# Retention followed by an MLP mixer on one core: the wide product of batches 2 and 3 by seven block products, and the narrow product's seven with fewer sums outside PSUM

## The chip, the core and the metric

The kernel runs on one core of a Trainium2 chip. The core has a matrix engine (TensorE, PE in the profile), VectorE (DVE), ScalarE (ACT), GpSimd (POOL) and SyncE (SP), which run their own instruction streams and wait for each other through semaphores. Matmul results land in PSUM, which has eight banks of 128 x 512 float32; everything else lies in SBUF. The metric is device time in microseconds (us).

## What is computed

Four batches, eight heads, 768 steps, head width 64. First a recurrent retention, then an MLP mixer over tokens (768 to 256 to 768) and over channels (512 to 1536 to 512):

```python
for t in range(S):
    state = gamma[None, :, None, None] * state + np.einsum('bhd,bhe->bhde', k[:, :, t], v[:, :, t])
    y[:, :, t] = scale * np.einsum('bhd,bhde->bhe', q[:, :, t], state)
...
xt = x.transpose(0, 2, 1)                     # x: y with its heads side by side
h = np.maximum(xt @ w_tok1, 0.0) @ w_tok2
u = x + h.transpose(0, 2, 1)
h2 = np.maximum(u @ w_ch1, 0.0) @ w_ch2
return (u + h2).astype(np.float32)
```

`u @ w_ch1` is called the wide product here (512 to 1536 channels), `relu(...) @ w_ch2` the narrow one.

## The kernel before, in words

**Fronts.** For each batch b and pair of heads p (four pairs), `front` (L470) does the retention in six chunks of 128 steps and the token mixer: it scales k and q by their decay (L498, L500), turns k and q (L522, L524 on PE, or a DMA transpose on SP, L512), sums the states between chunks (L553 on PE, L563 and L565 on DVE, L573 and L575 for the cast r), multiplies q by k under a mask (L589; the masked copy `am`, L615 on DVE, or L602 on ACT with L607 on POOL), adds up y (L626, L634), and mixes tokens (L657, L677). It leaves u in float32 in X and in float16 in u16 (L644, L701), and u16 is turned into uT, [128 channels, 4, 768 tokens], by a DMA transpose (L715) or by PE.

**Backs.** For each batch, `back` (L739) has these steps. `widen(sh)` (L750), for each half of the tokens: for each of 12 tiles of 128 wide channels, four matmuls of 384 columns into one bank (L760), emitted two by two, then a relu into h by ACT (L776). h is one buffer of [128, 12, 384] for each half, and there are two such buffers. `narrow7(i0, i1)` (L816) takes two blocks of 128 tokens and multiplies [2 token blocks x 1536] by [1536 x 512] as 2 x 2 blocks with seven products instead of eight: sums of h blocks (`hs`, L835, DVE), sums of w_ch2 blocks (`wsum`, L944, once), seven products of six matmuls of 256 columns (L850) into halves of three banks, and the recombination by DVE sums (L867): partial sums kept in SBUF in `us`, and sums into X. After that ACT issues the output's DMA (L904). All four batches take seven products in the narrow step, except that the last two token blocks of batch 3 use the plain `narrow` (L783, matmuls at L797, sums at L806).

**What sets the order.** Each piece of work is an `Op` with the engines that may do it, planned costs, dependencies, and the buffers it takes and uses. `arrange` (L94) plans all of it as a list schedule: each engine takes the first ready op in the order of a written-out rank (PRECEDENCE, L251), with rooms of each buffer kind (BUFS, L311) and PSUM banks (BANKS, L313: fronts take banks 0 to 5, backs 4 to 7, those of batch 0 banks 3 to 7). Where an op may go to one of several engines, the plan takes the one that it expects to end first, with 800 ns added to DVE after 30 us. The program is emitted in the planned order, so at run time each engine's order is fixed. Loads are issued by POOL in the order of the list ORDER (L918), except the first k by SP; until 21 us, idle PE time is filled with matmuls on zeros (L967).

Buffers before, one line of the code (name = number of rooms):

```python
BUFS = dict(kf=1, k=4, q=4, v=4, k16=3, q16=2, kT=4, qT=4, U=2, r16=3, am=8, X=3, x16=4, h1=5, u16=3,
            uT=2, h2=2, hs=2, us=2)
```

Of the kernel before, what the change touches and what calls it, by code (L numbers as in the profile page):

```python
# [9 lines left out]
FP = mybir.dt.float32  # L10
# [12 lines left out]
class Op:  # L23
# [3 lines left out]
    def __init__(self, ops, prio, ways, deps=(), takes=(), uses=(), dma=None, after=(), behind=None, guard=0):  # L27
        self.prio, self.ways, self.dma, self.guard = prio, ways, dma, guard
        self.deps = [d for d in deps if d is not None]
        self.after = [d for d in after if d is not None]  # L30
        self.behind = behind
        self.takes = list(takes)
        for s in list(takes) + list(uses):
            s.users.append(self)
        self.n = len(ops)
        ops.append(self)
# [51 lines left out]
ENGINES = ("PE", "ACT", "DVE", "POOL", "SP")  # L88
FREE = dict(PE=300, ACT=2500, DVE=900, POOL=900, SP=750)


def arrange(ops, BUFS, BANKS, rank):
# [18 lines left out]
    landed = []  # L111
    t = 0.0
# [61 lines left out]
    while left:  # L174
        moved = False
        wake = INF
        for e in ENGINES:
# [4 lines left out]
            for o in w_:  # L182
# [20 lines left out]
                start[o.n], eng[o.n], begun[o.n], way_of[o.n], bank_of[o.n] = t, e, True, way, banks  # L203
                free[e] = t + way[1]
                if o.dma:
                    rings.add(e, o, t)
                    if e == "SP":
                        free[e] = max(t + way[1], rings.made["SP"][-3])
                else:
                    end[o.n] = t + way[2]  # L210
# [41 lines left out]
    "a7sobxu4amg9691jmwlfv8dy40jegv0id1brctk2abu22jwa1o7wcwi9h93p4srd0d3w8z9rvbq63zkynbegkm53vwm682qhecai0qwnjiny"  # L252
    "6nprc04c3ucqralmiummeyb9an4n58b6fsmlu929r9r74bbudiadx1m2skajdlbaujjjnpww4m8bki9ebfapry52pfu0ugt0jsvc6g17dwb3"
    "7kgwngc1pca2kpg5l7bwr6nlagfg7ti81022rpax5gwvubvokoayl9itr57lt4n3lglkm5sl1efl0htbr15w6qwh3ghrpn9uale6789q5hqy"
    "e4mnn1iefv9bk5cv328p3s5zaa0cv3ke38usjwbh2eiqw39kuyrbnaato05e0mf1p6s0irwzavh7iceoqw6fp07ol0tpp185wc25uxl49w97"
    "au1fligypb8xobtl8ludnw6ygon5a53ysy9gfd5tssq1lqa9w47js25o8tc6ci98t7lwhs6ikvq2dccbtm943obk6dqj6cuz5mv7bn1dfola"
    "rfc7r3lh30t2pkx50xncuiekcr0red64gb6o6sndfkoobg79lrqdixdh5kpxqk8oquj3rmt58d9hpuju939677hdbmph0n2u0odtjpjgj7ot"
    "63mbe76xohq5txtj3akx0j7v68wsd3gqhfjco9bs7a5dulv075fy1arqa1vfdgqfgjijwfmcrlp4af7y91ut5ve5gpjy74vyd9oxkw609s1p"
    "k8ha152q8krrpt1h494t6hnf3qg4encadz4uvh2lk1lywoddj2f7lj12ro72x4ur3e3r6l904z99h22ow7th5a86ckc3rk0t0zgla65i1ncz"
    "dbqcrj84upl5w248bv9yak4e9x953c1q76wt8emzszuf3np73d1r5yhjouowbjrzgr6rm1sq36s58v11rcjkm8ktuh8solco5cjb20nih8q8"  # L260
    "815ss97urhejg1ewv9wisd7m2zf6v26z1m4qdodj3jhpezfmumlolegas4chg888hmft9o8r6teuojpwee9ikn189jcjc53bx0p82sw9i3r0"
    "ah0e4jku4xds07emp5klvvfinkwduqhk2ttomawj2dq431cmb8e270s6plri37o762lvnq1c19vjd6k7fnfz3l6upy1vru8ivkial38moksr"
    "p9j8b2lxhgkb4yev0uhipgu5vu0kmq1i9dq98ghosnpq009mmu16t1lzq35bnsmd7b1zpmb0vr7ch0bisw4lqsguwmhvwxg69tbqdu5p9ft9"
    "03l1lsbl9cqi8f8afu5jdfpogfnecyopuvsa0bm46joy576k2foztdmvkhlt6b4gd0vlaspafeexi12acfmhe3gnaz0a0p7ig2drffae41o6"
    "mt14qn1xva02ggmsfqvprv7e73lddaip2nt6seqm5fh5u1w69l4io3iwuor43vpp0gtsvxsu0l4pucet243fp2r8nm8qilhuhte0jx7qw5si"
    "ikqpqa6vdnc98uifi0kr2vv11gi780tn51fj71o2hbsv7gcglnllel1sf5vdqqcd47nvini4javzwqtcqx65cearisksaclcl2hhqrfxa3q7"
    "kqtzj41um9613mwywlqo33rx27jneasmmed4wuefjldpk04osgs3aq44imawwk892hg3bt9po8l8f4uan8orbejf7smrpvtwfcbo3higvmk3"
    "4250x35r044h21qgti8cfrk63iwb0yioj5vibd2wvnc8dqhqttccj6h1dk2p46mje8s8ihc2gxdeaopjtrd74asbgcvgge4vhxoeno6wmxiy"
    "cpjdii7ftunzg7kzo1f8b1lpjmoad566fwj909gt4des8nf31bdv23a8n7ps13st2ch3jh0wmkgdd2058wnhtvi2mgk99vwpsfi6h4n0lunu"
    "83ql2kdxuw45kg3kqe87m71tp3qbfbkjhnt3e1r2o41yeqocbpw8bb7xpiuet8tqtgdme9miwecsgzpdf2jzrn92scovcl6au8oq7dmpw0n2"  # L270
    "qz7zbya0b5hy1k7n5qtkizmykcukcnrtibka6708cu56fhhc9n54ebj0tfm3idiv2rgin9pzpeod01gmj1vqh69znxuub7un8h0ffp35spn4"
    "w1jovsmont8jmfl67p06qv555xn6ehwgjrei28jv6mheepnrkdrg1lte2b2mcx5ulbon593tfave7hofkk6p4w393xta4fersjf0njogb4rw"
    "u6gh9ahzf9g0d87rjqkfreq00s0vv5nnhw8y2yc44ko5vtv4qt43jtosbcwrsxa46e4rv6bzs12x5lrshl26i5342ioiomtyk4x2shs75nu7"
    "m0gk1wgsu32g"
# [4 lines left out]
def kernel(  # L279
# [31 lines left out]
    BUFS = dict(kf=1, k=4, q=4, v=4, k16=3, q16=2, kT=4, qT=4, U=2, r16=3, am=8, X=3, x16=4, h1=5, u16=3,  # L311
                uT=2, h2=2, hs=2, us=2)
    BANKS = dict(first=range(0, 8), front=range(0, 6), back=range(4, 8), back0=range(3, 8))  # L313
    SEVEN = (0, 1, 2, 3)
    CLIP = (2, 3)
# [46 lines left out]
    gq = const_p.tile([P, NP, S // 2], FP, name="gq")  # L362
    since = const_p.tile([P, HC, P], FP, name="since")
# [3 lines left out]
    zero = const_p.tile([P, 384], F16, name="zero")  # L367
    g128 = [(1.0 - 2.0 ** (-5.0 - h)) ** P for h in range(H)]

    def prep(eng, cost, emit, deps=(), prio=(-20, 0, -1)):  # L370
        return Op(ops, prio, [(eng, cost, cost + 40, emit)], deps)
# [12 lines left out]
    lgs_op = prep("DVE", 900, emit, [away_op])  # L384
# [9 lines left out]
    def emit():  # L394
        nc.gpsimd.iota(since, pattern=[[0, HC], [1, P]], base=-MID, channel_multiplier=0,
                       allow_small_or_imprecise_dtypes=True)
    since_op = prep("POOL", 500, emit)
# [5 lines left out]
    lnh_op = prep("DVE", 600, emit)  # L403

    def emit():
        for p in range(NP):
            nc.scalar.activation(gq[:, p], since.rearrange("p i t -> p (i t)"), AF.Exp, bias=lnsc, scale=lnh[:, p:p + 1])
    gq_op = prep("ACT", 1900, emit, [since_op, lnh_op, lgs_op], (-20, 0, -1, 1))
# [5 lines left out]
    gp_op = prep("DVE", 600, emit, prio=(-20, 0, -1, 2))  # L414
# [9 lines left out]
    wc1 = [const_p.tile([P, NP, FW * P], F16, name=f"wc1_{i}") for i in range(3)]  # L424
    wc2 = const_p.tile([P, NF, C], F16, name="wc2")
    N2, K2 = C // 2, NF // 2
    wsum = const_p.tile([P, 4, K2, N2], F16, name="wsum")
    wops = {}
# [20 lines left out]
    def load(b, p, what):  # L449
# [3 lines left out]
        s = Slot("kf" if hard else what)  # L453
# [16 lines left out]
    def front(b, p):  # L470
# [4 lines left out]
        def op(ways, deps=(), takes=(), uses=(), late=0, behind=None):  # L475
# [3 lines left out]
            return Op(ops, pr, ways, deps, takes, uses, guard=200 if pe and not first else 0, behind=behind)  # L479
# [28 lines left out]
        def turn(src, dst, dep, mode):  # L508
# [17 lines left out]
            t = op(one("PE", (340, 500), emit), dep + [ident_op], [T], [src])  # L526
            if mode == "w":
                def emit():
                    d = tile_of(dst, [P, S], F16).rearrange("d (f p c) -> d f p c", f=2, c=NC)
                    o = T.tile[:, :S].rearrange("d (c f p) -> d f p c", f=2, c=NC)  # L530
                    w = gq[:, p:p + 1].rearrange("d o (p c) -> d o p c", c=NC).to_broadcast([P, 2, SH // NC, NC])
                    nc.vector.tensor_tensor(d, o, w, ALU.mult)
                return op(one("DVE", (870, 950), emit), [t, gq_op], [dst], [T])
# [21 lines left out]
        pp = op(one("PE", (290, 450), emit), kl + [vl, two_before], [ST], [K, V])  # L555
# [20 lines left out]
        rs = op(either(emit, ACT=(455, 555), POOL=(450, 510), DVE=(235, 320)), [prev], [RS], [US])  # L576
# [14 lines left out]
        if first:  # L591
            a2 = [op(one("PE", (200, 350), lambda f=emit, h=hf: f([h])), [kt, qt, two_before],
                     A4[2 * hf:2 * hf + 2], [KT, QT]) for hf in range(2)]
        else:
            a2 = 2 * [op(one("PE", (360, 480), lambda f=emit: f([0, 1])), [kt, qt, two_before], A4, [KT, QT])]
# [40 lines left out]
        y2 = op(one("PE", (200, 360), emit), [rs, kt, qt, y0], [], [QT, RS] + Y)  # L636
# [102 lines left out]
    def back(b):  # L739
# [10 lines left out]
        def widen(sh):  # L750
            H2 = H2s[sh]
            rel = []
            for ft in range(NF):
                A = Slot(BA)

                def emit(cts, sh=sh, ft=ft, A=A):
                    acc = tile_of(A, [P, 512], FP) if cts[0] == 0 else A.tile
                    w = wc1[ft // FW]
                    for ct in cts:
                        nc.tensor.matmul(acc[:, :SH], w[:, ct, (ft % FW) * P:(ft % FW + 1) * P],  # L760
# [20 lines left out]
            rels.append(rel)  # L781

# [33 lines left out]
        def narrow7(i0, i1):  # L816
# [23 lines left out]
            opened = set()  # L840

            def product(g, half, left, right, deps):
                opens = g not in opened
                opened.add(g)

                def emit():
                    acc = tile_of(banks[g], [P, 512], FP) if opens else banks[g].tile
                    l, r = left(), right()
                    for j in range(K2):
                        nc.tensor.matmul(acc[:, half], l[:, j], r[:, j], start=(j == 0),  # L850
                                         stop=(j == K2 - 1))
                return op(one("PE", (650, 810), emit), deps, [banks[g]] if opens else [],
                          [ha, hb, HS] if opens else [ha, hb, HS, banks[g]])

# [7 lines left out]

            def add(dst, a_, b_, deps, uses, takes=()):
                def emit(e):
                    if US.tile is None:
                        tile_of(US, [P, 3, N2], FP)
# [80 lines left out]
    for b in range(B):  # L947
        for p in range(NP):
            front(b, p)
# [50 lines left out]
```

## Time and profile before

| | |
|---|---|
| time, median of 3 runs | 197.39 us (196.89 to 197.91) |
| the profiled execution | 197.98 us, of it span 196.0 us |
| instructions | 5761 |
| busy: PE, PEld (weight loads), DVE, ACT, POOL | 185.5, 137.9, 130.6, 119.8, 86.5 us |
| wide matmuls L760 / narrow matmuls L850 | 384 / 462 |
| granted TensorE clock | 1.00 throughout |

The page splits the span into 40 slices of 4.9 us; a digit is an engine's busy share of a slice in tenths. A row of a group gives line, engine, operation, tile written and tiles read, shape, count, then busy time, mean ns of one, and the idle time before them with what ended it. A matmul's ns is its duration from start to modelled end; in a stream matmuls overlap, so the spacing of starts is shorter. The chain of waits is the path followed back from the last instruction; its pieces are start, duration, engine, tile, line. The view of busy time by stages gives, for each stretch, its length, busy time of PE, PEld, DVE, ACT and POOL with instruction counts, the granted clock, and DMA.

### The profile page before, as it was taken

The numbers are of one execution on the slowest core, as the hardware profiler recorded it, in microseconds if no ns is written. First come the engines' busy times: TensorE is split into PE (matmuls) and PEld (weight loads), VectorE is DVE, ScalarE is ACT, GpSimd is POOL, SyncE is SP. The second block draws the span as 40 slices with busy tenths as digits, with TensorE's granted clock in tenths as the row PEclk, the third lists the DMA queues.
The fourth block names the chain that finished last, engine by engine and source line by source line (L and its number), as shares of the span: only waits on it lengthen the run. The fifth ranks groups of instructions, "written<-read, shape, count | busy, mean of one in ns | idle before, by whom it ended". The sixth has DMA issues, their size and how long they took to land.

```text
span 196.0 us, 5761 instructions
## 1 busy us (share of the span) xinstructions
PE 185.5 (95%) x2374; PEld 137.9 (70%) x2374; DVE 130.6 (67%) x356; ACT 119.8 (61%) x266; POOL 86.5 (44%) x112
## 2 busy tenths in 40 slices
PE   7879689999999999899999999999999999999993
PEld 3447578666678898667569888865579976667772
DVE  6799785465999999830379999704239993006981
ACT  3852569987798456399789454788774404674000
POOL 8993679624677527672454883134302100000000
PEclk9999999999999999999999999999999999999999
DMA  6999999999999999999978799992200443000124
GB/s 107 155 184 187 177 203 173 185 193 189 137 156 133 139 168 186 164 215 185 142 76 82 138 169 164 258 125 40 43 0 3 147 113 146 0 0 3 54 107 161
DMA packets 94233, 25.53 MB, mean 130 GB/s; under 512 B 84352, under 2 KB 91264, under 8 KB 94208
## 3 DMA queue, kind: packets, MB, share of 16 engines
q0 software_dynamic: 67456, 13.18, 83.2%
q1 hardware_dynamic: 23152, 5.71, 20.9%
q10 hardware_dynamic: 3600, 6.29, 10.5%
q8 instruction: 18, 0.29, 0.6%
q14 instruction: 7, 0.06, 0.1%
HBM read 26.74 MB, written 6.29 MB: 169 GB/s over the span
## 4 chain that ended last, share of the span: by engine, by line
PE 73%; DVE 9%; DMA 5%; issue 4%; POOL 3%; ACT 3%; POOLq 0%; DVEq 0%
PE bank L760 31%; PE bank L850 20%; PE bank L677 4%; PE bank L657 4%; DMA k<-in_k_dram 3%; PE bank L589 3%; PE bank L797 2%; PE bank L626 2%; DMA uT<-u 2%; DVE U L565 2%; DVE hs L835 2%; PE bank L634 2%; PE bank L553 2%; DVE am L615 1%; POOL r L575 1%
## 5 line engine op out<-in xcount | busy, mean ns | idle before, releaser
L760 PE MATMUL bank<-uT,wc 128*128 128x384 f16 x384 | 69.7, 326 | 0.5 <-DMA uT<-u 0.5
L776 ACT ACTIVATE h<-bank 128x384 f16<-128x384 f32 x96 | 45.2, 494 | 20.5 <-PE bank L760 13.5
L760 PEld LDWEIGHTS <-wc 128*128 128x128 f16 x384 | 34.9, 98 | 20.7
L615 DVE TENSOR_TENSOR am<-bank,mask 128x384 f16<-128x384 f32 x48 | 24.6, 551 | 10.2 <-PE bank L589 10.1
L850 PEld LDWEIGHTS <-hs 128*128 128x128 f16 x264 | 25.0, 98 | 3.8 <-DVE hs L835 0.2
L701 POOL CAST u<-X 128x384 f16<-128x384 f32 x23 | 12.4, 561 | 34.3 <-issue 17.8
L850 PE MATMUL bank<-wsum,hs 128*128 128x256 f16 x198 | 26.2, 273 | 0.0
L867 DVE TENSOR_TENSOR X<-X,bank 128x256 f32<-128x256 f32 x55 | 21.6, 417 | 1.9 <-PE bank L850 1.3
L835 DVE TENSOR_TENSOR hs<-h 128x768 f16<-128x768 f16 x18 | 10.1, 568 | 18.7 <-ACT h L776 18.7
L850 PEld LDWEIGHTS <-h 128*128 128x128 f16 x198 | 18.8, 98 | 3.7 <-issue 0.7
L460 POOL DMA_DIRECT2D v<-in_v_dram x16 | 16.6, 1037 | 8.5 <-PE bank L626 5.1
L575 POOL TENSOR_SCALAR r<-U,gp 128x320 f16<-128x320 f32 x11 | 13.0, 1179 | 14.7 <-DVE U L565 13.5
L565 DVE SCALAR_TENSOR_TENSOR U<-U,gp,bank 128x64 f32<-128x64 f32 x64 | 17.8, 278 | 1.6
L867 DVE TENSOR_TENSOR X<-X,us 128x256 f32<-128x256 f32 x44 | 18.4, 441 | 0.2
L850 PE MATMUL bank<-wc,h 128*128 128x256 f16 x132 | 17.7, 273 | 0.0
L563 DVE COPY U<-bank 128x64 f32<-128x64 f32 x16 | 3.5, 221 | 20.9 <-PE bank L553 20.7
L644 ACT COPY X<-bank 128x384 f32<-128x384 f32 x31 | 14.2, 485 | 5.4 <-PE bank L677 5.3
L644 ACT CAST x<-bank 128x384 f16<-128x384 f32 x32 | 14.4, 481 | 4.9 <-PE bank L634 2.5
L460 POOL DMA_DIRECT2D k<-in_k_dram x15 | 15.7, 1048 | 0.8 <-ACT h L776 0.7
L677 PE MATMUL bank<-h,wt 128*128 128x64 f16 x384 | 15.2, 193 | 0.7 <-ACT h L666 0.7
L677 PEld LDWEIGHTS <-wt 128*128 128x128 f16 x384 | 13.9, 98 | 2.4 <-issue 0.9
L498 ACT ACTIVATE k<-k,gk 128x384 f16<-128x384 f16 x22 | 12.8, 612 | 0.9 <-DMA k<-in_k_dram 0.8
(71 smaller groups left out, 257.6 us busy)
## 6 DMA issues: line engine op xcount, KB each, us to landing
out_dram<-X ACTq DMA_DIRECT2D x23, 256.0 KB, 2.9
q<-in_q_dram POOLq DMA_DIRECT2D x16, 192.0 KB, 8.4
v<-in_v_dram POOLq DMA_DIRECT2D x16, 192.0 KB, 8.2
k<-in_k_dram POOLq DMA_DIRECT2D x15, 192.0 KB, 7.6
wc<-in_moe_w_ch_dram POOLq DMA_DIRECT2D x5, 512.0 KB, 11.8
wt<-in_moe_w_tok_dram POOLq DMA_DIRECT2D x2, 384.0 KB, 8.8
wc<-in_moe_w_ch_dram POOLq DMA_DIRECT2D x2, 256.0 KB, 10.3
kf<-in_k_dram SPq DMA_DIRECT2D x1, 384.0 KB, 3.6
```

The source lines that it names most:

```text
L460: (nc.sync if hard else nc.gpsimd).dma_start(out=tile_of(s, [P, 2, NC, D], FP if hard else F16), in_=src.rearrange("h (c p) d -> p (h c) d ...
L498: nc.scalar.activation(t, src.tile[:, j], AF.Copy, scale=g[:, h:h + 1])
L565: nc.vector.scalar_tensor_tensor(out=u[:, c], in0=u[:, c - 1], scalar=gp[:, p:p + 1], in1=st, op0=ALU.mult, op1=ALU.add)
L575: (nc.vector if e == "DVE" else nc.gpsimd).tensor_scalar(r, u, g, None, ALU.mult)
L615: nc.vector.tensor_tensor(am, src, mask.to_broadcast([P, HC, P]), ALU.mult)
L644: (nc.scalar.copy if e == "ACT" else nc.vector.tensor_copy)(tile(), cols(src.tile[:, :S // 2]))
L677: nc.tensor.matmul(Y[j].tile[:, i * D:(i + 1) * D], wt2[:, jt, t], H1.tile[:, jt, j * D:(j + 1) * D], start=False, stop=(jt == NJ - 1), sk ...
L760: nc.tensor.matmul(acc[:, :SH], w[:, ct, (ft % FW) * P:(ft % FW + 1) * P], UT.tile[:, ct, sh * SH:(sh + 1) * SH], start=(ct == 0), stop=(c ...
L776: nc.scalar.activation(H2.tile[:, ft], A.tile[:, :SH], AF.Relu)
L835: (nc.vector if e == "DVE" else nc.gpsimd).tensor_tensor(HS.tile[:, j], x(), y(), f)
L850: nc.tensor.matmul(acc[:, half], l[:, j], r[:, j], start=(j == 0), stop=(j == K2 - 1))
L867: (nc.vector if e == "DVE" else nc.gpsimd).tensor_tensor(dst(), a_(), b_(), ALU.add)
```

## The change

1. **Wide product of batches 2 and 3** (`WIDE7`): a new `widen7` does both token halves at once as a 2 x 2 x 2 block product (two halves of the 512 channels, two halves of the 1536, two halves of the tokens) with seven products instead of eight. It needs four sums of uT blocks (`ts`, a batch) and four sums of wc1 blocks (`AS`, once). Each of six blocks i covers tiles i and i + 6 of both halves. One bank (R1) gathers four products on top of each other, and is copied out after each of the first three into `ks`; R2 gathers two products, R3 holds one. Three outputs are a bank plus a kept copy, written to h by DVE and clipped in place by DVE or POOL; the fourth is clipped straight out of R1.
2. **Narrow product**: the same seven products, with four of them gathered in one bank in the same manner (`chain`, `keep`: three copies into `us`) and two in another (`tail`). Of the sums outside PSUM six are left, two of which (y11; y2, over both halves of X's row) may go to POOL.
3. **Room**: `wc1` is one tile instead of three; the table `gq` and `AS` share one buffer (`late`), the first k and `since` use `us`; there are fewer rooms for k16, kT, qT, am, x16 and h1.
4. **Order**: other ranks, another order of the loads, and in the planner new costs for some ops and a time for PE's changes between tile shapes (`tiled`).

The diff, cut to its core (ranks and planner costs left out):

```diff
-    BUFS = dict(kf=1, k=4, q=4, v=4, k16=3, q16=2, kT=4, qT=4, U=2, r16=3, am=8, X=3, x16=4, h1=5, u16=3,
-                uT=2, h2=2, hs=2, us=2)
+    BUFS = dict(late=1, k=4, q=4, v=4, k16=2, q16=2, kT=3, qT=3, U=2, r16=3, am=6, X=3, x16=3, h1=3, u16=3,
+                uT=2, h2=2, hs=2, us=2, ts=1, ks=2)
+    WIDE7 = (2, 3)
...
-    wc1 = [const_p.tile([P, NP, FW * P], F16, name=f"wc1_{i}") for i in range(3)]
+    wc1 = const_p.tile([P, NP, NF * P], F16, name="wc1")
...
+        def widen7():
...
+            sums = [(u(0, hi), u(0, lo), None), (u(1, hi), t(0), 0), (u(1, hi), u(0, hi), None), (u(1, lo), t(1), 1)]
...
+                def product(R, left, right, deps, first, extra):
+                    def emit():
+                        acc = tile_of(R, [P, 512], FP) if first else R.tile
+                        r = right()
+                        for ct in range(C2):
+                            nc.tensor.matmul(acc[:, :SH], left(ct), r[:, ct], start=first and ct == 0,
+                                             stop=ct == C2 - 1, skip_group_check=True)
...
+                def keep(j, dep):
+                    def emit(e):
+                        ks = tile_of(KS, [P, 3, SH], FP) if j == 0 else KS.tile
+                        (nc.scalar.copy if e == "ACT" else nc.vector.tensor_copy)(ks[:, j], R1.tile[:, :SH])
...
+                def out_of(R, j, dep, k, m, sh):
+                    def emit():
+                        nc.vector.tensor_tensor(h(m, sh), R.tile[:, :SH], KS.tile[:, j], ALU.add)
+                    opens = not rel
+                    ad = op(one("DVE", (465, 548), emit), [dep, k] + list(rel.values())[:1],
+                            list(H2s) if opens else [], [R, KS] + ([] if opens else [H2s[sh]]))
+                    def emit(e):
+                        (nc.vector if e == "DVE" else nc.gpsimd).tensor_scalar(h(m, sh), h(m, sh), 0.0, None, ALU.max)
+                    rel[i + m * M2, sh] = op(either(emit, DVE=(180, 260), POOL=(460, 520)), [ad], [], [H2s[sh]])
...
+                p1 = product(R1, weights(4), u(0, lo), ready + cw, True, [UT])
+                k1 = keep(0, p1)
+                p2 = product(R3, weights(5), u(1, lo), ready + cw, True, [UT])
+                out_of(R3, 0, p2, k1, 0, 0)
+                p6 = product(R1, weights(1), t(1), [ts[1], k1] + asums, False, [TS])
+                k2 = keep(1, p6)
+                p7 = product(R2, weights(2), t(2), [ts[2]] + asums, True, [TS])
+                p5 = product(R1, weights(0), t(0), [ts[0], k2] + asums, False, [TS])
+                k4 = keep(2, p5)
+                a22 = out_of(R2, 2, p7, k4, 1, 1)
+                p4 = product(R2, weights(7), t(3), [ts[3], a22] + cw, False, [TS])
+                out_of(R2, 1, p4, k2, 1, 0)
+                p3 = product(R1, weights(3), u(1, hi), [k4] + asums, False, [UT])
...
         def narrow7(i0, i1):
...
-            u0 = op(either(emit, ACT=act(N2), DVE=dve(N2)), [p1], [US], [banks[0]])
-            p2 = product(2, lo, lambda: h(ha, ta, 1), w(1, lo), ra[K2:] + cw)
-            y1 = add(part(x0, lo), part(x0, lo), u(0), [u0] + xd, [US, X])
-            o11 = add(part(x0, lo), part(x0, lo), acc(2, lo), [p2, y1], [X, banks[2]])
-            p6 = product(0, hi, lambda: HS.tile[:, 1], t(1), [sm[1], u0] + wsums)
-            u2 = add(u(1), u(0), acc(0, hi), [u0, p6], [US, banks[0]])
-            p5 = product(1, lo, lambda: HS.tile[:, 0], t(0), [sm[0]] + wsums)
-            y3 = add(part(x1, lo), part(x1, lo), u(1), [u2] + xd, [US, X])
-            p4 = product(2, hi, lambda: h(hb, tb, 1), t(3), rb[K2:] + wsums + [o11])
-            u4 = add(u(2), u(1), acc(1, lo), [u2, p5], [US, banks[1]])
-            z3 = add(part(x1, lo), part(x1, lo), acc(2, hi), [p4, y3], [X, banks[2]])
-            p7 = product(1, hi, lambda: HS.tile[:, 2], t(2), [sm[2], u4] + wsums)
-            y2 = add(part(x0, hi), part(x0, hi), u(2), [u4] + xd, [US, X])
-            y4 = add(part(x1, hi), part(x1, hi), u(2), [u4] + xd, [US, X])
...
+            k1 = keep(0, p1)
+            p2 = tail(2, lambda: h(ha, ta, 1), w(1, lo), ra[K2:] + cw, True)
+            o11 = add(part(x0, lo), acc(2, lo), [p2] + xd, [X, banks[2]], FROM_BANK)
+            y11 = add(part(x0, lo), u(0), [k1, o11], [US, X], FROM_KEPT)
+            p6 = chain(lambda: HS.tile[:, 1], t(1), [sm[1], k1] + wsums, False, False)
+            k2 = keep(1, p6)
+            p7 = tail(1, lambda: HS.tile[:, 2], t(2), [sm[2]] + wsums, True)
+            o22 = add(part(x1, hi), acc(1, lo), [p7] + xd, [X, banks[1]], FROM_BANK)
+            p5 = chain(lambda: HS.tile[:, 0], t(0), [sm[0], k2] + wsums, False, False)
+            k4 = keep(2, p5)
+            p4 = tail(1, lambda: h(hb, tb, 1), t(3), rb[K2:] + wsums + [o22], False)
+            o21 = add(part(x1, lo), acc(1, lo), [p4], [X, banks[1]], FROM_BANK)
+            y2 = add(x1, lambda: US.tile[:, 1:3].rearrange("p a b -> p (a b)"), [k4, o21, o22], [US, X],
+                     dict(DVE=(606, 690), POOL=(1150, 1230)))
+            p3 = chain(lambda: HS.tile[:, 3], w(1, hi), [sm[3], k4] + cw, False, True)
+            o12 = add(part(x0, hi), acc(0, lo), [p3] + xd, [X, banks[0]], FROM_BANK)
...
-    ORDER = ("q00 k00 k03 v00 k01 q01 k02 q02 t1 v01 q03 t2 v02 a0 v03 k10 a3 q10 a2 a1 k11 v10 k12 q11 "
-             "v11 b0 v12 b1 q12 b2 k13 v13 q13 k20 v20 v21 q20 q21 k21 k22 v22 k23 q22 q23 v23 k30 v30 q30 "
+    ORDER = ("q01 k00 q02 q00 k01 v00 k02 k03 v01 v02 t1 q03 t2 v03 a0 q10 k10 q11 k11 a1 v10 v11 q12 a3 "
+             "v12 k12 a2 b1 b0 b2 k13 v13 q13 k20 v20 v21 q20 q21 k21 k22 v22 k23 q22 q23 v23 k30 v30 q30 "
...
+    parts = [(lambda: aw(0, 1), lambda: aw(1, 1), ALU.add, None), (lambda: AS.tile[:, 0], lambda: aw(0, 0), ALU.subtract, 0),
+             (lambda: aw(0, 0), lambda: aw(0, 1), ALU.subtract, None), (lambda: aw(1, 0), lambda: AS.tile[:, 1], ALU.subtract, 1)]
+            nc.vector.tensor_tensor(AS.tile[:, j], x(), y(), f)
```

## The prediction

> **What bounds the kernel now.** I read the slices of the page first, then the chain that ended last, then busy time by stages, then rows and single instructions. All times are us.
>
> ```profile
> PE 185.5 (95%) x2374; PEld 137.9 (70%) x2374; DVE 130.6 (67%) x356; ACT 119.8 (61%) x266; POOL 86.5 (44%) x112
> PE   7879689999999999899999999999999999999993
> DVE  6799785465999999830379999704239993006981
> PEclk9999999999999999999999999999999999999999
> ```
>
> TensorE is full from slice 7 (about 30) to slice 39 (about 192); VectorE (DVE) is full only in three stretches. A busy PE can hide slack, so I checked with spacings. The chain of waits, in order of time, has the last batch's wide product as one unbroken piece, and by line it is mostly two PE lines:
>
> ```profile
> PE bank L760 31%; PE bank L850 20%; PE bank L677 4%; PE bank L657 4%; DMA k<-in_k_dram 3%; PE bank L589 3%; PE bank L797 2%; PE bank L626 2%; DMA uT<-u 2%; DVE U L565 2%; DVE hs L835 2%; PE bank L634 2%; PE bank L553 2%; DVE am L615 1%; POOL r L575 1%
> ...
> 163.33 14.62 PE bank L760 x90
> ```
>
> So a wide matmul (384 columns) costs 14.62/90 = 0.1624 of PE in a stream, not the 0.326 that its row gives as one instruction's duration. The same chain has 6 narrow matmuls of 256 columns in 0.65, 0.109 each. I multiplied each PE group's count per 5 us by such spacings: every stretch from 35 to 160 holds 4.8 to 5.3 us of matmul work but 80 to 85 (4.3). TensorE sets the time there; only its work, or a new wait in it, changes the end. Busy time by stages shows the company it keeps:
>
> ```profile
> 163.00:178.00 15.00, 15.00 (x96) 9.15 (x94) 0.89 (x3) 10.45 (x23) 0.00 (x0) 1.00 0.10 36
> 178.00:192.00 14.00, 14.00 (x118) 11.30 (x117) 12.30 (x31) 1.40 (x4) 0.00 (x0) 1.00 0.21 79
> 50.00:80.00 30.00, 30.00 (x446) 24.61 (x445) 28.91 (x74) 21.23 (x47) 18.79 (x23) 1.00 2.02 156
> ```
>
> The columns are PE, PEld, DVE, ACT, POOL. While batch 3 is widened DVE is idle and ACT works 10.45 of 15; where narrow products run DVE is nearly full. The rows I price with:
>
> ```profile
> L776 ACT ACTIVATE h<-bank 128x384 f16<-128x384 f32 x96 | 45.2, 494 | 20.5 <-PE bank L760 13.5
> L615 DVE TENSOR_TENSOR am<-bank,mask 128x384 f16<-128x384 f32 x48 | 24.6, 551 | 10.2 <-PE bank L589 10.1
> ...
> L867 DVE TENSOR_TENSOR X<-X,bank 128x256 f32<-128x256 f32 x55 | 21.6, 417 | 1.9 <-PE bank L850 1.3
> ...
> L867 DVE TENSOR_TENSOR X<-X,us 128x256 f32<-128x256 f32 x44 | 18.4, 441 | 0.2
> ```
>
> **Part 1, the wide product of batches 2 and 3.** Removed: 96 matmuls a batch (12 tiles, 2 halves, 4 steps). Added: 6 blocks of 7 products of 2, so 84. That is 12 x 2 = 24 matmuls of the same shape fewer, **-3.9** (24 x 0.1624), on the engine that sets the end. ACT copies 18 partial sums and clips 6 results a batch, 24 x 0.494 = 11.9, the same as its 24 clips before. New on DVE a batch: 4 differences of uT (768 f16, the shape of the hs sums, 0.554) = 2.2, and 18 bank-plus-kept sums into h, which no row shows; the row nearest is am (bank with an SBUF operand, 384 into f16), 0.551, the bounds are 0.417 (256 columns) and 0.8 (its size doubled): 18 x 0.551 = 9.9. The 18 clips in place go to POOL or DVE: POOL's nearest row is the 384-wide f16 select, 0.52 (0.5 to 0.85 over rows), DVE's the 384-wide f16 scaling, 0.315 at its median. In batch 2 this lies beside batch 3's front, where DVE was busy 6.12 of 120 to 130 and 2.37 of 130 to 140: covered. In batch 3 it is PE 84 x 0.1624 = 13.6, ACT 11.9, DVE 12.1 (17.8 if DVE clips as well): PE stays longest only if POOL does the clips, which is free there.
>
> What waits: one bank takes p1, p6, p5, p3 in turn, with a copy after each of the first three and a clip at the end: 4 x (0.162 + 0.326 + 0.494 + about 0.06 of hand-over, my estimate from gaps of 0.03 to 0.16 in the stage's order of time) = 4.2 a block. Six blocks one after the other would be 25; PE's 13.6 needs 25/13.6 = 1.85 chains side by side. The second bank (p7, sum, p4, sum) is held 2.2 to 2.8, the third 1.1: 7.5 to 8.1 bank-us a block over the four back banks, 1.9 to 2.0 against PE's 2.27. It fits with about a tenth to spare. h is two buffers, both taken at the first sum, so batch 2's narrow products can't fill in under batch 3's blocks. At the exit the last block's p4, sum, clip (0.49 + 0.55 + 0.52) and two hs sums (1.1) run before the first product of sums; PE has p3, p1, p2 (0.33 + 0.65 + 0.65) for it: about 1.0 bare. At the entry p6 needs two differences (1.1) after the last uT, beside p1, p2 and k1. I take **+1.3** for entry, exit and imperfect overlap (bounds 0.3 and +5, the latter 1.4 chains).
>
> **Part 2, the narrow product** (11 pairs). 42 matmuls a pair before and after: 0 on PE. Before, a pair's DVE work is 4 x 0.554 + 5 x 0.417 + 4 x 0.441 + 2 x 0.416 = 6.9 against PE's 42 x 0.109 = 4.6. After: 2.2 + 4 x 0.417 = 3.9, with one 256-wide and one 512-wide SBUF sum (0.44 and about 0.9) on DVE or POOL: 3.9 to 5.2, so 19 to 33 off DVE in all; ACT gets two copies of 0.372 a pair, 8.2 in all, where it was busy 21 of 30. As PE was full in these stretches, little of this reaches the end: PE's gaps after 30 are about 1.3, the largest 0.67 at 80 to 90 and 0.46 at 160 (a uT transfer). I take **-0.3** (bounds -1.3 and +1). POOL's two-input sums have no row: at least DVE's 0.44 and 0.9, at most the 1.5 of its slowest row (r, 320 elements) twice over; behind them stand load issues of about 1.0 each and the casts of u, which the uT transfers wait for.
>
> The POOL rows bear on that. At 104.08 one r took 1.49 against a median of 1.085, and the two-input hs sum that ran into it 0.81 against 0.554:
>
> ```profile
> 104.08 1.49 POOL L575 TENSOR_SCALAR r<-U,gp 128x320 f16<-128x320 f32 x1 [1.01 <-DVE U L565]
> ```
>
> ```profile
> 104.62 0.81 DVE L835 TENSOR_TENSOR hs<-h 128x768 f16<-128x768 f16 x1
> ```
>
> [...]
>
> **Part 3, the rest.** Four sums of wc1 (as wsum's, 0.954 each) put 3.8 on DVE once, needed at about 125 and possible from the last scaled q of batch 1 on: hidden by what part 2 frees; uncovered, up to +3.8. Loads: batch 0's are a permutation among themselves; two weight pieces land later, two q and two k of batch 1 earlier. PE was 7.99, 8.72 and 7.48 busy in the first three tens, filler included: 0, bounds -1 and +1.5. Fewer buffers (am 8 to 6, h1 5 to 3, kT and qT 4 to 3, x16 4 to 3, k16 3 to 2) let fewer fronts run at once: nothing where PE is full of other work, a part of the +1.5 at the start. One wc1 tile in place of three adds no work.
>
> **Sum.** The profiled execution ran 197.98 (span 196.0 and 2.0 around it). 197.98 - 3.9 + 1.3 - 0.3 = 195.1. It lies 0.6 above the median of 197.39, so **194.5** for a median.
>
> **Rivals.** (a) DVE's relief does reach the end, because stretches where PE and DVE are both full (50 to 80, 100 to 120) hide small PE stalls: -1.3 in place of -0.3, 193.0 to 193.5. For it: DVE 28.91 of 30. Against: matmul counts by spacing fill the same stretches. (b) The saving is eaten: start (+1) from fewer buffers, and waits of +2.5 to +3.5 in the two wide stages: 196.5 to 198. For it: all 84 products wait for a copy, a sum or a bank, and the order is fixed in advance, so slips add up. Against: narrow products already wait so, with PE full. (c) **Slower**: batch 3's blocks don't overlap, because the first bank's chain and the four banks let 1.25 chains run on average: 25.2/1.25 = 20.2 against 15.6 before, +4.6, less batch 2's 1.95, with 1.0 bare: 201. It decides below about 1.5 chains (16.8 + 1.0 = 15.6 + 1.95 + 0.3). (d) Also slower: fronts of batches 1 to 3, with fewer buffers, come late to uT and open PE gaps as at 160, 0.5 to 1 for each of 4: 198.5 to 200. That the 24 matmuls stay can be excluded by the loops.
>
> **How the numbers follow.** A difference of under 0.5%, about 1.0 us, can't be told from no change here. Chances: forecast (193.5 to 196.3) 0.48, (a) 0.10, (b) 0.18, (c) 0.15, (d) 0.09. Faster 0.58, same 0.18, slower 0.24. The range 192.6 to 198.8 takes in (a), (b) and the near side of (c) and (d).
>
> **What would show it.** Wide matmuls 384 to 360 and 24 x 0.162 less PE; batch 3's wide stage 14 to 15 with PE without gaps over 0.3, DVE at 12 in it; DVE's adds per pair near 4; the last front's uT about 2 us earlier. Wrong if PE shows gaps released by ks copies (ACT) or the sums into h (DVE) that add up to over 2.5, if wide starts later than 35, or if POOL's two-input sums run over 1.5 and casts of u queue behind them.

## The result, and the profile after

The changed kernel takes **212.69 us** (median of 4 runs, 211.12 to 213.12) against 197.65 before in the same session: ratio **1.076** (95% interval 1.072 to 1.080), 15 us slower. The forecast was 194.5 and the range ended at 198.8. The profiled execution ran 212.27, span 210.3. Some executions of a kernel run one per cent or more longer at a lower granted clock (in e3 212.65 at 0.976, the other three 208.95 to 209.34 at 0.984 to 1.000), and the times of the runs below leave them out (one of e3's four, two of e8's four). The kernel before took 197.0 to 197.7 (medians) in the five sessions, so less than about 1 us between runs of different sessions says little.

The same lines of the page as before, of the changed kernel:

```profile
PE 188.5 (90%) x2348; PEld 137.2 (65%) x2348; DVE 137.0 (65%) x335; ACT 127.7 (61%) x293; POOL 136.6 (65%) x157
PE   7979898999979988999999998997699989955993
POOL 8985774517344957660179837899978348997041
PEclk9999999999999997599999999999999999999699
```

PE now has holes, the deepest at slices 29, 36 and 37; POOL's busy time went from 86.5 to 136.6; and the granted clock falls in slices 16 and 17 (0.50 from 82.0 to 88.8) and again in slice 38 (0.50 from 194.6 to 198.0, behind the last hole). In the chain of waits a POOL line stands second, and in order of time its last long piece is one row of clips:

```profile
PE bank L770 14%; POOL h L859 13%; PE bank L984 6%; DVE hs L948 6%; PE bank L994 5%; PE bank L834 5%; DMA q<-in_q_dram 3%; DVE X L1001 3%; DMA k<-in_k_dram 3%; PE bank L688 3%; PE bank L668 3%; DVE ts L809 3%; DVE am L626 2%; PE bank L637 2%; DVE U L575 2%
```

```profile
175.27 17.00 POOL h L859 x15
192.29 0.56 DVE hs L948
```

By the groups of the same profile (busy us, mean ns), a clip takes 1179 ns, twice the select of the same size and type that I had priced it by; the row behind these three is of the kernel before, POOL's operation of the same name there, of only 320 elements:

```profile
L859 POOL TENSOR_SCALAR h<-h 128x384 f16<-128x384 f16 x35 | 40.3, 1179 | 3.8 <-DVE h L853 3.8
L1001 POOL TENSOR_TENSOR X<-X,us 128x256 f32<-128x256 f32 (+1 forms) x20 | 21.5, 1074 | 27.3 <-DVE X L1001 18.1
L618 POOL TENSOR_SCALAR_AFFINE_SELECT am<-am 128x384 f16<-128x384 f16 x16 | 8.9, 572 | 7.4 <-ACT am L613 7.4
```

```profile
L575 POOL TENSOR_SCALAR r<-U,gp 128x320 f16<-128x320 f32 x11 | 13.0, 1179 | 14.7 <-DVE U L565 13.5 <-PE bank L524 1.2
```

The shortest of POOL's 35 clips took 1161 ns, and the last five or so ran while DVE stood idle (6.09 us before 192.29), so waiting for DVE is not what makes them long.

The starts of the first wide product of batches 1, 2 and 3, and the end of the span, place the loss:

| | batch 1 | batch 2 | batch 3 | end |
|---|---|---|---|---|
| before | 80.7 | 125.7 | 160.6 | 196.0 |
| changed | 87.0 | 126.6 | 167.7 | 210.3 |
| e6 (below) | 83.2 | 123.0 | 160.2 | 194.8 |

There are two losses: ahead of batch 1 (+6.3), and in the stages with the new wide product (41.1 and 42.6 where 34.9 and 35.4 were). Against the kernel before, whose order is another, only 0.9 of the first is left at batch 2; against e6, whose planned order is the changed kernel's, the 3.8 at batch 1 are still 3.6 at batch 2.

### The profile page after: what moved, and what is told of

Same layout as the page of the kernel before. It is cut to its first block, busy times and chain, and to the rows that moved or that the text cites. A ratio compares the mean times of both kernels' runs of the same rounds, so it can differ in the third digit from the quotient of the medians.

```text
span 210.3 us, 5786 instructions
## 1 busy us (share of the span) xinstructions
PE 188.5 (90%) x2348; PEld 137.2 (65%) x2348; DVE 137.0 (65%) x335; ACT 127.7 (61%) x293; POOL 136.6 (65%) x157
## 4 chain that ended last, share of the span: by engine, by line
PE 45%; DVE 21%; POOL 19%; DMA 7%; issue 4%; ACT 2%; POOLq 0%; DVEq 0%; ACTq 0%
PE bank L770 14%; POOL h L859 13%; PE bank L984 6%; DVE hs L948 6%; PE bank L994 5%; PE bank L834 5%; DMA q<-in_q_dram 3%; DVE X L1001 3%; DMA k<-in_k_dram 3%; PE bank L688 3%; PE bank L668 3%; DVE ts L809 3%; DVE am L626 2%; PE bank L637 2%; DVE U L575 2%
## 5 line engine op out<-in xcount | busy, mean ns | idle before, releaser
L859 POOL TENSOR_SCALAR h<-h 128x384 f16<-128x384 f16 x35 | 40.3, 1179 | 3.8 <-DVE h L853 3.8
L1001 POOL TENSOR_TENSOR X<-X,us 128x256 f32<-128x256 f32 (+1 forms) x20 | 21.5, 1074 | 27.3 <-DVE X L1001 18.1
L626 DVE TENSOR_TENSOR am<-bank,mask 128x384 f16<-128x384 f32 x48 | 24.6, 549 | 21.6 <-PE bank L599 20.9
L770 PE MATMUL bank<-uT,wc 128*128 128x384 f16 x192 | 35.4, 332 | 0.0
L974 ACT COPY us<-bank 128x256 f32<-128x256 f32 x33 | 12.2, 374 | 26.7 <-PE bank L984 26.5
L853 DVE TENSOR_TENSOR h<-bank,ks 128x384 f16<-128x384 f32 x36 | 19.5, 554 | 11.1 <-PE bank L834 7.8
L786 ACT ACTIVATE h<-bank 128x384 f16<-128x384 f32 x48 | 22.0, 494 | 7.4 <-PE bank L770 7.1
L770 PEld LDWEIGHTS <-wc 128*128 128x128 f16 x192 | 17.9, 100 | 11.0 <-issue 0.9
L842 ACT COPY ks<-bank 128x384 f32<-128x384 f32 x36 | 16.6, 482 | 8.0 <-PE bank L834 5.7
L948 DVE TENSOR_TENSOR hs<-h 128x768 f16<-128x768 f16 x18 | 11.1, 625 | 12.1 <-POOL h L859 7.1
L984 PE MATMUL bank<-wsum,hs 128*128 128x256 f16 x132 | 17.4, 273 | 1.3 <-DVE hs L948 1.3
L834 PE MATMUL bank<-ts,late 128*128 128x384 f16 x72 | 15.9, 326 | 0.0
L508 ACT ACTIVATE k<-k,gk 128x384 f16<-128x384 f16 x21 | 12.6, 623 | 5.4 <-DMA k<-in_k_dram 4.1
```

The lines of the kernel that those rows point to most:

```text
L626: nc.vector.tensor_tensor(am, src, mask.to_broadcast([P, HC, P]), ALU.mult)
L770: nc.tensor.matmul(acc[:, :SH], wc1[:, ct, ft * P:(ft + 1) * P], UT.tile[:, ct, sh * SH:(sh + 1) * SH], start=(ct == 0), stop=(ct == NP - 1))
L786: nc.scalar.activation(H2.tile[:, ft], A.tile[:, :SH], AF.Relu)
L834: nc.tensor.matmul(acc[:, :SH], left(ct), r[:, ct], start=first and ct == 0, stop=ct == C2 - 1, skip_group_check=True)
L859: (nc.vector if e == "DVE" else nc.gpsimd).tensor_scalar(h(m, sh), h(m, sh), 0.0, None, ALU.max)
L948: (nc.vector if e == "DVE" else nc.gpsimd).tensor_tensor(HS.tile[:, j], x(), y(), f)
```

## The experiments

Theory A: POOL's clips pace the new wide product. Rivals: B, order and rooms; C, DVE; D, POOL's and DVE's two-input sums shut each other out, a conjecture; the nearest rows are the prediction's pair at 104 (an r on POOL of 1.49 against 1.085, an hs sum on DVE beside it of 0.81 against 0.554). E and F came later, for the stretch from 64 to 90. Unless said otherwise an edit changes only the engine or the place at which an operation is emitted; the planned order of all else stays.

**e1, e2: the clips.**

```diff
-(nc.vector if e == "DVE" else nc.gpsimd).tensor_scalar(h(m, sh), h(m, sh), 0.0, None, ALU.max)
+nc.vector.tensor_scalar(h(m, sh), h(m, sh), 0.0, None, ALU.max)     (e1; e2: pass)
```

> All 36 clips in place (L859) issued by DVE instead of POOL, each at the place that the plan gave it; all else as in the changed kernel. Theory A (POOL's clip of 1.18 us, not the planned 0.5, paces the wide stages of batches 2 and 3): 36 x 1.18 leave POOL, the 17 us run of clips at 175 to 192 goes, and the stage from the first wide product of batch 3 to the last output shrinks from 42.6 to about 35; about 201 to 204 in all. Theory B (the order and the smaller buffers are the cause, POOL's clips only fill time that PE waits anyway): within 2 us of 212.7. Theory C (DVE then becomes the bound, at 0.9 us a clip as the one clip that DVE has now): 209 to 212.

> The 36 clips in place are left out altogether, so three of the four blocks of h of batches 2 and 3 are not clipped; all else as in the changed kernel. Gives the whole price of the clips with no other engine paying. Theory A: 199 to 202, a little under the kernel with clips on DVE. Theory B: within 2 us of 212.7. Under both what stays above 197.4 is owed to something else (narrow stage of batch 0, clock).

Measured: e1 **201.60** (ratio 1.020, 1.012 to 1.027), e2 199.85. Theory A; B and C fall. The clips cost 11.1 us on POOL compared with DVE, 12.8 in all; the second fall of the clock, which e1's profile does not have, is part of that (six matmuls of 256 columns took 1.46 in it, at 194.61, and 0.83 just ahead of it, at 193.84). Busy time in the clip stretches (PE, PEld, DVE, ACT, POOL), first of the changed kernel, then of e1 with its row of clips:

```profile
140.00:150.00 10.00, 8.28 (x99) 5.02 (x97) 6.49 (x15) 7.44 (x19) 10.00 (x13) 1.00 0.11 21
180.00:190.00 10.00, 7.66 (x45) 4.18 (x44) 3.72 (x7) 4.48 (x11) 10.00 (x10) 1.00 0.00 0
```

```profile
140.00:150.00 10.00, 9.77 (x114) 5.97 (x112) 9.68 (x29) 8.89 (x21) 3.05 (x6) 1.00 0.11 22
170.00:180.00 10.00, 9.62 (x58) 5.50 (x57) 9.42 (x26) 6.88 (x16) 0.86 (x1) 1.00 0.16 59
```

```profile
L859 DVE TENSOR_SCALAR h<-h 128x384 f16<-128x384 f16 x36 | 9.8, 284 | 0.6
```

POOL was full while DVE and ACT had room; on DVE a clip takes a quarter of the time (0.284 against 1.179), and PE is nearly full again.

**e3, e4: the sums of X and kept copies.** `nc.vector` in `add` in place of the choice; e3 with clips on POOL, e4 with clips on DVE.

> The 20 sums of X and kept copies that POOL does in the narrow product are issued by DVE at the same places; clips stay on POOL. Theory A: the tail is unchanged, so the time stays above 208. Theory D (POOL's sums and DVE's two-input sums shut each other out, which stretches the narrow stage of batch 0 and lets the clock fall at 82): the first wide product of batch 1 comes back from 87.0 to 81 to 83, the clock stays at 1.00 there, and the time falls by 3 to 6 to 207 to 210. If DVE simply has too much to do there, the first wide product of batch 1 comes later than 87.

> Both the clips and the sums on DVE: POOL does nothing that it did not do before. Theories A and D together: the gains of the two add up, 196 to 200. Theory B: over 205 still.

Measured: e3 209.09 (1.060, 1.054 to 1.066), e4 **200.06** (1.013, 1.006 to 1.021). Together the two edits gain 12.6, less than the 3.6 and 11.1 that each gains alone. What D expects of DVE's sums is there, but not where I put it: e3 takes the first wide product of batch 1 from 87.0 to 86.4 only, though the clock stays at 1.00 there in its profile. Where it shows is ts (count, then ns min/median/max), changed kernel and then e3:

```profile
L809 DVE TENSOR_TENSOR ts<-uT,ts x4: 550/1066/1618, 127.1 to 168.5; 128x768 f16<-128x768 f16 x4
```

```profile
L809 DVE TENSOR_TENSOR ts<-uT,ts x4: 551/552/553, 126.7 to 167.7; 128x768 f16<-128x768 f16 x4
```

A two-input DVE sum took up to three times its time beside POOL's sums of X, and 0.55 without them: the one of 1.62 started at 128.36, while a sum of X held POOL from 128.00 to 129.56. What makes it longer there is not shown.

**e5, e6, e7: the four sums of wc1 later**, held back in the emission until the sixteenth pair of batch 1's wide matmuls; e5 on the changed kernel, e6 on e4, e7 on e1.

> The four sums of wc1 blocks (late, 3.8 us of DVE) are issued after the sixteenth pair of batch 1's wide matmuls (about 90), where DVE has nothing to do, instead of at 68 to 81; clips and sums stay on POOL. Theory E (between 64 and 83 DVE is full and sets the time, and these sums stand in front of the masks and states of batch 1's last fronts): the first wide product of batch 1 moves from 87.0 to 81 to 83, the clock no longer falls at 82, the time falls by 4 to 7 to 206 to 209. Rival F (fewer buffers or the load order set that stretch): within 1.5 us of 212.7.

> Clips and sums of X on DVE, and the four sums of wc1 late: theories A, D and E together. If they are all that went wrong, what is left is the 24 matmuls less: 193 to 196, faster than before. If F holds as well, 198 to 200.

> Clips on DVE, sums of X on POOL, the four sums of wc1 late: tells whether POOL is of any use for the sums of X. If POOL's sums relieve DVE, this is faster than the kernel with both on DVE by 1 to 2 us; if they shut DVE out, slower by 1 to 2 us (the pair without the late sums was 201.6 against 200.1).

Measured: e5 208.00, **e6 196.74** (0.997, 0.991 to 1.003), e7 198.04. Theory E: 4.7, 3.3 and 3.6 faster than their fellows. In e4 DVE is full from 64 to 83 and these sums stand inside (first and last shown). In e6 DVE does them from 83.5 to 87.5, earlier than the expected 90 but right behind that stretch (second view of it), with PE full beside them:

```profile
64.00:83.00 19.00, 16.33 (x264) 13.07 (x264) 18.69 (x42) 10.37 (x25) 10.23 (x13) 0.97 1.51 168
```

```profile
68.30 0.95 DVE L1078 TENSOR_TENSOR late<-wc 128x1536 f16<-128x1536 f16 x1
...
79.98 0.94 DVE L1078 TENSOR_TENSOR late<-wc,late 128x1536 f16<-128x1536 f16 x1
```

```profile
64.00:83.00 19.00, 17.88 (x323) 14.83 (x320) 17.30 (x46) 12.81 (x31) 11.55 (x16) 1.00 1.64 163
```

```profile
83.54 0.95 DVE L1078 TENSOR_TENSOR late<-wc 128x1536 f16<-128x1536 f16 x1
...
86.26 1.26 DVE L1078 TENSOR_TENSOR late<-wc,late 128x1536 f16<-128x1536 f16 x1
```

e7 against e6 says that POOL's sums of X cost 1.3 and bring nothing at the end. e6 misses the 193 to 196 that was expected if theories A, D and E were all that went wrong.

**e14: the clock.** e4 with four groups of matmuls of batch 1's fronts issued twice (one of the three loops changed is shown).

```diff
-            for jt in range(NJ):
+            for jt in (2 if (b, p) in ((1, 1), (1, 2)) else 1) * list(range(NJ)):
```

> As e4_both_dve, but in four places of batch 1's fronts, where PE then waits for DVE (69 to 80), matmuls are issued twice over (the token mixer's first product of pairs 1 and 2, the state products of pair 3, the scores of pair 1; each restarts its sum, so the result is the same): 2.1 us more PE work and no other change. If the fall of the granted clock at 82 to 89 follows from PE's idle time before it and costs by itself: the clock stays at 1.00 and the time falls from 200.1 to 197 to 199. If DVE alone sets that stretch: 200 to 202.

Measured: 200.80 (1.017, 1.012 to 1.021), inconclusive: the doubled matmuls left PE idle for 1.5 of the 4 us from 78 to 82 (1.7 in e4), and the clock fell all the same, for less long (3.4 us). In e4 the clock was halved (0.50) from 81.8 to 88.6:

```profile
80.00:85.00 5.00, 4.17 (x79) 3.20 (x78) 3.80 (x8) 3.87 (x10) 3.75 (x7) 0.68 1.93 178
85.00:90.00 5.00, 5.00 (x57) 3.85 (x56) 2.77 (x8) 3.29 (x7) 2.59 (x3) 0.64 1.51 152
```

But e4's four executions differ: 200.95 at a mean clock of 0.980, 200.69 at 0.997, 199.43 at 0.999, 198.82 at 1.000. If the last is e4 without the fall, the clock is some 1.2 of the 3.3 and DVE's work 2.1; that split is argued from four executions, not shown, and the 200.69 at 0.997 speaks against it.

**e8, e12: the rooms.** e8 is the kernel before with the smaller rooms; e12 is e10 (next) with the old ones.

> The kernel before with the changed kernel's rooms for k16, kT, qT, am, x16 and h1 (2, 3, 3, 6, 3, 3), planned anew with its own ranks. Theory E: the rooms matter little, 197 to 199. Rival F: PE gets gaps in the fronts at the start and between 60 and 90, 200 to 205.

> The kernel of e10_wide8, which has no ts, ks and sums of wc1 and so has space, with the old rooms for k16, kT, qT, am, x16 and h1 (3, 4, 4, 8, 4, 5), planned anew with the same ranks. If the smaller rooms held its PE up: 198 to 202, two or more under its 204.2. If the changed kernel's ranks were found for the small rooms and use no more: within 1 of 204.2.

Measured: e8 219.1 (1.109, 1.098 to 1.120, two executions); e12 205.47 against e10's 204.20. With ranks found for the larger rooms the smaller ones cost some 22 us, more than either theory expected; with ranks found for the smaller ones, the larger ones bring nothing. Rooms and ranks belong together; of the changed kernel's own loss, rooms are no part that these runs show.

**e9, e10, e11: each part by itself.** e9 is e6 told to the planner, which then sets a new order; e10 is e9 with `WIDE7 = ()`; e11 is the kernel before with the new narrow product alone.

> As the kernel with clips and sums on DVE and the four sums of wc1 late, but told to the planner (clip DVE only, 235 to 315 ns; sums of X DVE only; the sums of wc1 after the sixteenth pair of batch 1's wide matmuls), so that the order of all engines is worked out anew from the same ranks. If the order made for wrong costs was part of the loss: 193.5 to 196, faster than the 196.7 of the one that kept the old order. If the ranks, searched for the wrong costs, don't fit: 197 to 201.

> The kernel of e9_replanned with the plain wide product for all batches (24 matmuls more, no ts, no ks, no sums of wc1), ranks of the plain product's pieces laid into the places of the seven's. Prices the wide change alone under one set of rooms: if the 24 matmuls are worth their 3.9 us, 3 to 5 slower than e9_replanned; if sums and clips on DVE eat them, within 1; ranks made for the other may add 1 to 3.

> The kernel before with the new narrow product alone (sums of X on DVE), old rooms and old ranks, planned anew. By the prediction's part 2 the narrow change is worth about nothing at the end (-0.3, bounds -1.3 and +1): 196 to 198.5. If its fewer DVE sums do reach the end: 194 to 196. If its longer chain through one bank stalls PE: over 199.

Measured: e9 200.53 (1.018, 1.014 to 1.022), e10 204.20, e11 199.38 (1.013, 1.009 to 1.016). e9 does the same work as e6 in another order and is 3.8 slower: the order weighs as much as the 24 matmuls. e10 is 3.7 slower than e9. In e11 DVE lost what was worked out, yet the end came 2.4 later, clear of its interval and in that branch of the expectation where the longer chain stalls PE. The groups of sums before (the third; the prediction shows the other two, 21.6 and 18.4) and in e11:

```profile
L867 DVE TENSOR_TENSOR us<-us,bank 128x256 f32<-128x256 f32 x22 | 9.2, 416 | 0.3 <-PE bank L850 0.2
```

```profile
L889 DVE TENSOR_TENSOR X<-X,bank 128x256 f32<-128x256 f32 x44 | 18.1, 416 | 12.3 <-PE bank L882 8.7 <-PE bank L872 3.6
L889 DVE TENSOR_TENSOR X<-X,us 128x512 f32<-128x512 f32 (+1 forms) x22 | 12.3, 558 | 4.1 <-ACT us L862 3.7
```

PE's idle time from 70 to 90 is 1.9 in e11 where it was 0.7 before, and one of its waits there (0.53 at 78.1) ends with a copy out of the chain's bank. But e11's order is new too, so 199.38 doesn't price the product alone, and how much of the 2.4 is the chain stays open.

**e13: the clips on ACT.** e6 with `nc.scalar.activation(h(m, sh), h(m, sh), AF.Relu)`.

> As e6_dve_late, but the 36 clips in place issued by ACT at their places instead of DVE. DVE gets 9 us back, ACT pays 36 x about 0.4 to 0.5 (an estimate from its 256-wide and 384-wide rows, 0.37 and 0.49). If DVE paces batch 2's wide stage: 194 to 196. If ACT, which already does the copies that each bank's chain waits for, becomes the pace: 198 to 202.

Measured: 201.25 (1.020, 1.017 to 1.023). A clip takes ACT 0.559, and ACT, which also does the copies in the banks' chain, becomes the pace (columns as above, ACT fourth):

```profile
L859 ACT ACTIVATE h<-h 128x384 f16<-128x384 f16 x36 | 20.1, 559 | 2.7 <-DVE h L853 2.7
```

```profile
140.00:150.00 10.00, 8.77 (x109) 5.41 (x108) 6.41 (x14) 10.00 (x27) 2.09 (x4) 1.00 0.11 23
170.00:180.00 10.00, 9.36 (x52) 4.92 (x51) 5.95 (x11) 10.00 (x26) 0.00 (x0) 1.00 0.07 26
```

No version beats the kernel before clear of its interval; e6 and e7 are even with it.

## Why the prediction was wrong

**The step that failed** is part 1's price of a clip: "POOL's nearest row is the 384-wide f16 select, 0.52 (0.5 to 0.85 over rows)". It measured 1.18 (median 1.17). The nearer row was in the same table: r<-U, a tensor-scalar operation on POOL, 1.085 at its median for only 320 elements; I took likeness of size and type over likeness of operation. I also never multiplied: my own upper bound, 18 x 0.85 = 15.3, was already more than PE's 13.6. With 18 x 1.17 = 21 a batch against these 13.6 the sentence "PE stays longest only if POOL does the clips, which is free there" turns round: POOL is what the stage waits for. e1 puts that at 11.1 us and e2 at 12.8. All my rivals for the stage were chains of banks; none was POOL itself. My signs of being wrong looked there too, at gaps of PE behind the copies (ACT) and the sums into h (DVE); in the changed kernel the new products' matmuls waited 0.4 for these sums, while the narrow product's waited 8.4 for POOL's clips.

**The second failed step** is part 3's sums of wc1, "hidden by what part 2 frees; uncovered, up to +3.8". They were planned into 68 to 81, where DVE was full: 3.3 to 4.7 (e5 to e7), part of it perhaps the clock, which I had taken as 1.00 throughout. **Third**, part 2 put nothing in the sum for POOL's sums of X: they cost 3.6 in e3 and 1.3 in e7 against e6.

One after the other, from the changed kernel to e1, e7 and e6, the three are worth 11.1, 3.6 and 1.3. That is 16.0 of the 18.2 by which the forecast missed; the 2.2 between e6 and the forecast are not explained by these runs.

**What held.** The wide product's main term is borne out, but not proved: e10 gives 3.7 for 24 matmuls where 3.9 was worked out, and e10's ranks are not its own, which its expectation put at 1 to 3. That blocks can overlap held: in e6's chain 56 of batch 3's 84 matmuls are one piece, 0.173 each against 0.1624 in a stream, so rival (c) with its 1.25 chains falls:

```profile
165.77 9.70 PE bank L834 x56
```

The narrow product's relief of DVE: e11's sums take 30.4 where before took 49.2, 18.8 less, and 19 was the figure with all on DVE; that this doesn't make the end earlier held, and rival (a) falls. That smaller rooms cost little held, as far as e8 and e12 show, only with ranks found for them.

**What stays open.** e6 has none of the three faults and 24 matmuls less, and only ties. PE's idle time between 30 and 192 grew by about as much as the 24 matmuls are worth (the column behind the length is PE), before and then e6:

```profile
30.00:192.00 162.00, 160.71 (x1988) 120.93 (x1985) 105.99 (x275) 103.61 (x236) 63.54 (x82) 1.00 1.10 123
```

```profile
30.00:192.00 162.00, 156.26 (x1908) 116.26 (x1908) 121.06 (x306) 108.95 (x255) 50.69 (x70) 1.00 1.08 126
```

1.3 idle before, 5.7 in e6 (some 0.5 of it behind its last matmul), spread over many short waits at 30 to 40, 60 to 90 and 110 to 130. Whether an order searched with the true costs would close them was not tried; e9, planned with them but with the old ranks, was slower than e6.

## What to carry to other kernels

Price an operation on an engine by that engine's row of the same operation, and let size come second. When a change moves work to an idle engine, multiply its own rate by the count and set that against the stage, because an idle engine can still be the slowest there (here POOL, with 1.18 a clip against DVE's 0.27 to 0.28); and when a planner chooses the engine, a wrong cost in it becomes a wrong program. In these runs saved matmuls paid nothing where another engine was filled up by handing them over (POOL in the changed kernel, ACT in e13).

## What the runs showed of the hardware

One clip of 128 x 384 float16 in place took 1.18 on GpSimd, 0.27 to 0.28 on VectorE (e4, e1) and 0.56 on ScalarE (e13), on the mean. GpSimd's time is more than four times VectorE's. GpSimd's select of the same size and type at 0.57 (changed kernel) shows that the operation matters, not the engine alone.

From 78 to 82 PE stood idle for 1.4 of the 4 us in the changed kernel and 1.7 in e4, and then the granted clock was 0.50 for 6.8 us; a row of twelve token-mixer matmuls took 1.44 in it (changed kernel, 85.75) and 0.83 at full clock (e6, 82.53). PE stood idle as long in the profiles of e2 (1.4) and e3 (1.6), where the clock stayed at 1.00 to 89, and three other executions of e4 had a mean clock of 0.997 to 1.000: the idle time alone does not decide it. What does is not shown.
